# Attention scores on four row groups of the TensorE array, in three blocks per pair of heads

## The chip, the cores and the metric

The kernel runs on one core of a Trainium2 chip. The metric is the time of one execution on the device, in microseconds (us), as the median of three runs. A core has five engines that run their own instruction streams side by side and wait for one another by semaphores: TensorE (PE in the profile; its weight loads are shown apart as PEld), VectorE (DVE), ScalarE (ACT), GpSimd (POOL) and SyncE (SP), which here issues most of the DMA transfers.

## What is computed

Two stages. The first is attention restricted to equal hash buckets: a query sees the keys whose six sign bits under a random projection equal its own.

```python
batch, n_heads, seq, head_dim = (4, 8, 768, 64)
...
q_bits = (np.einsum('bhsd,dk->bhsk', q, proj) > 0).astype(np.int64)
k_bits = (np.einsum('bhsd,dk->bhsk', k, proj) > 0).astype(np.int64)
...
mask = q_bucket[:, :, :, None] == k_bucket[:, :, None, :]
scores = scale * np.matmul(q, k.transpose(0, 1, 3, 2))
scores = np.where(mask, scores, -1000000000.0)
scores = scores - np.max(scores, axis=-1, keepdims=True)
attn = np.exp(scores)
attn = attn / (np.sum(attn, axis=-1, keepdims=True) + 1e-09)
return np.matmul(attn, v).astype(np.float32)
```

The second stage takes the result as 3072 tokens of 512 numbers through a feed-forward block with 2048 hidden units and the quick form of gelu:

```python
h = x @ w_in
g = h * (1.0 / (1.0 + np.exp(-1.702 * h)))
return (g @ w_out).astype(np.float32)
```

All inputs and outputs are float32.

## The kernel before

Attention works on 16 pairs of heads (`pairs`, n = 0 to 15). The two heads of a pair lie in the two halves of the 128 partitions, 64 numbers of the head dimension each; j is the head within the pair. The 768 queries are taken in two halves c of 384 columns, the 768 keys in six tiles kt of 128. A PSUM tile `ps` spans two banks of 512 columns, one for each head.

The mask is not applied to scores. `hashed` (L405) multiplies projection and data and leaves the hash dots of q and k in one tile; `featured` (L414) turns their signs into bf16 numbers of size 2^16 in a small tile `f`, and eight DMA copies lay the rows of `f` out as features `feats[n % 2]`, 12 rows for each head. A product of these features is zero where all bits agree and hugely negative where one differs. `scores` (L426) adds both products in PSUM: for each key tile and head a bf16 matmul over the features (on 64 rows of the array, of which 12 hold numbers), then an f32 matmul over the head dimension (64 rows, and two passes on TensorE, each with its own weight load). The two heads use different halves of the array's rows. ScalarE then writes `es[c][:, kt]`, the exponential of the scaled sum (L436).

`values` (L453) multiplies v with these exponentials: 24 f32 matmuls for each c, each of 32 output columns of the array, four side by side. `unload` (L476) copies the result out of PSUM into `xT`. The sums of the exponentials over keys are made in two steps: `add_low` (L440) adds tiles 0 to 2 on GpSimd, `add_high` (L446) adds tiles 3 to 5 and the low sum on VectorE, and `total` (L482) adds over the 128 partitions with ones on TensorE, into `dn`. `invert` (L491) and `norm` (L507) divide by them on VectorE.

Data is prepared ahead: `fetch` (L320) loads q and k of pair n + 3, `turn` (L391) transposes those of pair n + 2 on VectorE, `measure` (L396) squares them on ScalarE and keeps the sum, for a check of sizes. Each pair also converts one chunk of the weights `w_in` (`convert`, L158: one 512 KB load `raw`, six steps on VectorE, one on ScalarE).

For a pair n from 1 on, the order is written out by hand. On TensorE: the scores of all six key tiles for c = 0, then for c = 1, then the values for c = 0 and for c = 1, the hash dots of pair n + 2, and the sums `total(n)`. The engines other than SyncE keep this order; SyncE's is made by the scheduler from it. In the profile of before SyncE issues, for each pair: eight feature copies (L423), the load of `raw` (L162), two loads of v (L343), four of k and four of q (L331). PSUM's eight banks are held by three pools: three places of two banks for `ps`, one bank for `av` and `dn`, one for hashes and the second `av`.

Of the kernel before, what the change touches and what calls it, by code (L numbers as in the profile page):

```python
# [38 lines left out]
def kernel(  # L39
# [246 lines left out]
    def attention(ff):  # L286
# [4 lines left out]
        with actx:  # L291
# [4 lines left out]
            aps = actx.enter_context(tc.tile_pool(name="aps", bufs=1, space=PSUM))  # L296
            mps = actx.enter_context(tc.tile_pool(name="mps", bufs=1, space=PSUM))
            early = actx.enter_context(ExitStack())
            ep = early.enter_context(tc.tile_pool(name="ep", bufs=1))
            sps = early.enter_context(tc.tile_pool(name="sps", bufs=GT, space=PSUM))  # L300
# [44 lines left out]
            def first_pair():  # L345
# [4 lines left out]
                for i, (name, src) in enumerate((("k", k), ("q", q))):  # L350
# [7 lines left out]
                    xts[0, name] = wk.tile([P, S], F32, tag=f"{name}T", name=f"{name}T")  # L358

                nc.scalar.activation(const.tile([1, 1], F32, name="first"), ones[0:1, 0:1], Act.Exp)  # L360
                for _ in range(4):
                    nc.tensor.matmul(aps.tile([P, 512], F32, tag="av", name="warm"), idle[:, 0:P], idle, start=True, stop=True)
                hash_weights()

                def turned(name, c, move):
                    tp = sps.tile([P, 2, 512], F32, tag="s", name="tp")[:, 0, 0:HS]
                    for i in range(GT):
                        for j in range(2):
                            nc.tensor.matmul(tp[D * j : D * (j + 1), i * P : (i + 1) * P], x[name][:, j, c * GT + i, :], ident,  # L369
                                             start=True, stop=True)  # L370
                    move(xts[0, name][:, c * HS : (c + 1) * HS], tp)

                def bits(name, c):
                    cols = slice(c * HS, (c + 1) * HS)
                    h = sps.tile([P, 2, 512], F32, tag="s", name="hash0")[:, 0, 0:HS]
# [13 lines left out]
                return lambda: bits("q", 1)  # L389

            def turn(n, name):  # L391
                x = raws[n, name]
                xt = xts[n, name] = wk.tile([P, S], F32, tag=f"{name}T", name=f"{name}T")
                nc.vector.transpose(xt, x.rearrange("p s i -> p (s i)"))

# [9 lines left out]
            def hashed(n):  # L405

                h = dots[n] = mps.tile([P, HS], F32, tag="m", name="hash")
# [6 lines left out]
            def featured(n):  # L414
                f = wk.tile([P, HS], BF16, tag="f", name="f", bufs=1)
                nc.vector.tensor_scalar(f, dots.pop(n), above[:, 0:1], weight[:, 0:1], op0=Alu.is_gt, op1=Alu.mult)
                for c in range(2):
                    for i, x in enumerate("kq"):

                        queue = nc.scalar if (n, x, c) == (1, "q", 0) else nc.sync  # L420
                        for j in range(2):
                            r0 = D * i + 32 * c + 2 * NB * j
                            queue.dma_start(out=feats[n % 2][x][D * j : D * j + 2 * NB, c * HS : (c + 1) * HS],  # L423
                                            in_=f[r0 : r0 + 2 * NB, :])

            def scores(n, c, kts):  # L426
                qT, kT, qf, kf = xts[n, "q"], xts[n, "k"], feats[n % 2]["q"], feats[n % 2]["k"]
                cols = slice(c * HS, (c + 1) * HS)
                for kt in kts:
                    ps = sps.tile([P, 2, 512], F32, tag="s", name="ps")  # L430
# [5 lines left out]
                    nc.scalar.activation(es[c][:, kt, :, 0:HS], ps[:, :, 0:HS], Act.Exp, scale=1.0 / D**0.5)  # L436
# [3 lines left out]
            def add_low(n, c):  # L440

                acc = accs[n, c, 0] = st.tile([P, 2, HS], F32, tag="acc0", name="acc0", bufs=1)
                nc.gpsimd.tensor_tensor(acc, es[c][:, 0, :, 0:HS], es[c][:, 1, :, 0:HS], op=Alu.add)  # L443
                nc.gpsimd.tensor_tensor(acc, acc, es[c][:, 2, :, 0:HS], op=Alu.add)  # L444

            def add_high(n, c):  # L446
                e = [es[c][:, GT + i, :, 0:HS] for i in range(GT)]
                acc = accs[n, c] = st.tile([P, 2, HS], F32, tag="acc", name="acc")
                nc.vector.scalar_tensor_tensor(acc, e[0], T * TINY, e[1], op0=Alu.add, op1=Alu.add)  # L449
                for x in (e[2], accs.pop((n, c, 0))):  # L450
                    nc.vector.tensor_tensor(acc, acc, x, op=Alu.add)  # L451

            def values(n, c, kts):  # L453
                if 0 in kts:


                    if c and n == 0 or c and n + 2 > last:
                        avs[n, c] = mps.tile([P, HS + 1], F32, tag="m", name="av")
                    elif c:
                        avs[n, c] = sps.tile([P, 2, 512], F32, tag="s", name="av1")[:, 0, 0 : HS + 1]  # L460
                    else:
                        avs[n, c] = aps.tile([P, HS + 1], F32, tag="av", name="av")
                av, vt = avs[n, c], vts[n]
# [18 lines left out]
            def total(n):  # L482

                dn = accs[n] = aps.tile([P, HS], F32, tag="av", name="dn")
# [6 lines left out]
            def invert(n):  # L491
# [7 lines left out]
                for r0 in range(0, P, 32):  # L499
# [5 lines left out]
                                    r.rearrange("p c s -> p (c s)").unsqueeze(2).to_broadcast([P, S // 32, 32]))  # L505

# [19 lines left out]
            def guard(part):  # L526
                if part == 0:
                    nc.vector.tensor_reduce(largest, sizes, axis=AX.X, op=Alu.max)
                else:
                    row = mps.tile([1, P], F32, tag="m", name="row")  # L530
                    nc.tensor.transpose(row, largest, ident)
                    nc.vector.tensor_reduce(largest[0:1, 0:1], row, axis=AX.X, op=Alu.max)
# [7 lines left out]
            scores(0, 0, low)  # L540
            rest()
            add_low(0, 0)
            scores(0, 0, high)
            turn(1, "k")
            measure(1, "k")
            values(0, 0, low)
            fetch(2, "k")
            scores(0, 1, low)
            add_low(0, 1)
            add_high(0, 0)  # L550
            turn(1, "q")
            measure(1, "q")
            values(0, 0, high)
            unload(0, 0)
            hashed(1)
# [3 lines left out]
            scores(0, 1, high)  # L559
            measure(2, "k")  # L560
            values(0, 1, low)
            values(0, 1, high)
            unload(0, 1)
            for n in range(1, last + 1):

                scores(n, 0, every)
                add_low(n, 0)
                if n == 1:
                    add_high(0, 1)
                    for x in "kq":  # L570
                        turn(2, x)
                    fetch(3, "k")
                    total(0)
                    measure(2, "q")
                    fetch(3, "q")
                    fetch_v(2)
                whole(invert(n - 1))
                norm(n - 1)
                if n == last:
                    guard(0)  # L580
                scores(n, 1, every)
                add_low(n, 1)
                add_high(n, 0)
                if n == 1:
                    hashed(2)
                    featured(2)
                if n + 2 <= last:
                    for x in "kq":
                        turn(n + 2, x)
                        measure(n + 2, x)  # L590
                if n == last:
                    guard(1)
                add_high(n, 1)
                values(n, 0, every)
                unload(n, 0)
                step(n, 6)
# [3 lines left out]
                if 1 < n < last:  # L600
                    fetch_v(n + 1)
                values(n, 1, every)
                unload(n, 1)
                if n + 2 <= last:
# [750 lines left out]
```

## Time and profile before

| | |
|---|---|
| median of three runs | 857.03 us (857.01 to 857.36) |
| the profiled execution | 856.89 us, of which the span from first to last instruction is 855.1 us |
| TensorE busy | 846.1 us, 99% of the span |
| VectorE busy | 701.5 us, 82% |
| ScalarE busy | 345.1 us, 40% |
| GpSimd busy | 357.1 us, 42% |
| granted TensorE clock | 0.998 |

The profile shows one execution. A group's row gives the source line, the engine, the operation, the tiles written and read, the shapes, a count, the busy time and the mean duration in ns of one, and then the engine's idle time before them with what ended it. In shapes such as 64\*128 64x384 the first pair is rows and columns of the array, the second the moving operand. A timeline row starts with the start in us from the begin of the span and the time from the first start to the last end of the instructions merged in it. A windows row gives a stretch, its length and the busy time of each engine in it, with the number of instructions in brackets. The chain of waits is followed back from the last instruction to whatever released it. Matmuls overlap in the array, so a matmul's duration is longer than its share of the time: the distance between starts counts.

### The profile page before, as it was taken

What the parts mean: (1) busy time and instruction counts of PE and PEld (TensorE: products, weight loads), DVE (VectorE), ACT (ScalarE), POOL (GpSimd) and SP (SyncE); (2) the same over time, 40 slices, a digit from 0 to 9 for tenths busy, and PEclk for the clock granted to TensorE, in tenths of its full rate; (3) what the DMA queues carried; (4) which work ended last, traced back from release to release, by engine and by line L of the source; (5) the groups of instructions that cost most, each with busy time, mean ns of one, the idle gap of its engine ahead of it and who ended that gap; (6) DMA issues with size and microseconds to landing.
All of it is one profiled execution on the core that took longest, in us unless ns stands there. A gap on an engine that the chain in (4) does not pass through costs nothing.

```text
span 855.1 us, 13646 instructions
## 1 busy us (share of the span) xinstructions
PE 846.1 (99%) x5007; PEld 529.1 (62%) x5007; DVE 701.5 (82%) x1069; ACT 345.1 (40%) x549; POOL 357.1 (42%) x316
## 2 busy tenths in 40 slices
PE   8999999999999999999999999999999999999996
PEld 4444444444444444566666666545888888888885
DVE  4489999999999885788887788676998977897786
ACT  5866666777766654343444444433000000000000
POOL 4333333433333358997854466668664100000000
PEclk9999999999999999999999999999999999999999
DMA  5635654444563103436565536587844675467534
GB/s 128 94 58 103 105 101 85 85 86 86 108 112 77 48 26 135 159 103 243 197 221 222 222 147 231 187 274 263 288 164 157 205 248 192 159 214 240 191 114 100
DMA packets 160903, 132.07 MB, mean 154 GB/s; under 512 B 122656, under 2 KB 137664, under 8 KB 155584
## 3 DMA queue, kind: packets, MB, share of 16 engines
q1 hardware_dynamic: 152448, 106.89, 44.6%
q10 hardware_dynamic: 8384, 24.27, 8.2%
q8 instruction: 40, 0.66, 0.3%
q14 instruction: 31, 0.25, 0.1%
HBM read 79.69 MB, written 50.33 MB: 152 GB/s over the span
## 4 chain that ended last, share of the span: by engine, by line
PE 98%; DMA 1%; ACT 0%; DVE 0%; ACTq 0%; issue 0%; DVEq 0%
PE product L1078 30%; PE product L751 23%; PE ps L435 18%; PE av L468 15%; PE small L819 6%; PE product L819 3%; PE dn L489 1%; PE hash L411 1%; DMA q<-in_q_dram 1%; PE hash L376 0%; PE tp L369 0%; ACT c L764 0%; DVE v L767 0%; ACT size L190 0%; DVE y L1058 0%
## 5 line engine op out<-in xcount | busy, mean ns | idle before, releaser
L436 ACT ACTIVATE e<-ps 128x768 f32<-128x768 f32 x192 | 151.2, 812 | 26.2 <-PE ps L435 23.6
L435 PE MATMUL ps<-qT,kT 64*128 64x384 f32 x768 | 155.1, 482 | 0.0
L443 POOL TENSOR_TENSOR acc<-e 128x768 f32<-128x768 f32 x32 | 51.6, 1613 | 195.1 <-ACT e L436 174.8
L468 PE MATMUL av<-e,v 128*32 128x385 f32 x1536 | 128.0, 487 | 0.0
L751 PE MATMUL product<-xT,w_in_sb 128*128 128x512 f32 x216 | 100.1, 593 | 0.1
L468 PEld LDWEIGHTS av<-e,v 128*32 128x32 f32 x1536 | 48.5, 109 | 76.3 <-issue 74.6
L435 PEld LDWEIGHTS ps<-qT,kT 64*128 64x128 f32 x768 | 68.0, 187 | 38.4 <-issue 38.4
L751 PE MATMUL product<-t_x,s_in 128*128 128x512 f32 x192 | 89.4, 592 | 0.0
L1114 ACT COPY u<-product 128x256 f32<-128x256 f32 x20 | 7.4, 372 | 158.4 <-PE product L1078 125.2
L751 PEld LDWEIGHTS product<-xT,w_in_sb 128*128 128x128 f32 x216 | 40.9, 190 | 36.5 <-issue 33.3
L435 PE MATMUL ps<-qf,kf 64*128 64x384 bf16 x384 | 62.8, 323 | 0.1
L444 POOL TENSOR_TENSOR acc<-acc,e 128x768 f32<-128x768 f32 x32 | 55.8, 1745 | 2.5
L751 PEld LDWEIGHTS product<-t_x,s_in 128*128 128x128 f32 x192 | 36.5, 190 | 29.7 <-issue 26.8
L449 DVE SCALAR_TENSOR_TENSOR acc<-e 128x768 f32<-128x768 f32 x32 | 47.7, 1490 | 5.1 <-ACT e L436 5.1
L767 DVE TENSOR_TENSOR u<-product,u 128x256 f32<-128x256 f32 (+1 forms) x60 | 28.4, 486 | 16.3 <-PE product L819 13.0
L435 PEld LDWEIGHTS <-kf 64*128 64x128 bf16 x384 | 18.9, 94 | 35.2 <-DMA q<-in_q_dram 6.2
L451 DVE TENSOR_TENSOR acc<-acc,e 128x768 f32<-128x768 f32 x32 | 34.3, 1072 | 3.3
L451 DVE TENSOR_TENSOR acc<-acc,acc 128x768 f32<-128x768 f32 x32 | 31.2, 974 | 6.6 <-POOL acc L444 3.2
L1078 PE MATMUL product<-raw_g,xT 128*128 128x256 f32 x152 | 35.1, 379 | 0.0
L767 DVE TENSOR_TENSOR v<-product,v 128x512 f32<-128x512 f32 x24 | 16.5, 689 | 20.0 <-PE product L751 20.0
L223 POOL TENSOR_TENSOR v<-c,v 128x1024 f32<-128x1024 f32 (+1 forms) x15 | 32.3, 2156 | 1.0
L222 POOL TENSOR_TENSOR u<-v,u 128x1024 f32<-128x1024 f32 (+1 forms) x11 | 23.8, 2163 | 20.7 <-ACT size L190 8.1
(284 smaller groups left out, 1721.9 us busy)
## 6 DMA issues: line engine op xcount, KB each, us to landing
raw_g<-g_dram SPq DMA_DIRECT2D x20, 1024.0 KB
s_in<-g_dram SPq DMA_DIRECT2D x20, 1024.0 KB
g_dram<-c ACTq DMA_DIRECT2D x18, 512.0 KB
raw<-in_moe_w_out_dram ACTq DMA_DIRECT2D x16, 512.0 KB
raw<-in_moe_w_in_dram SPq DMA_DIRECT2D x15, 512.0 KB
v<-in_v_dram SPq DMA_DIRECT2D x32, 192.0 KB
k<-in_k_dram SPq DMA_DIRECT2D x60, 96.0 KB
q<-in_q_dram SPq DMA_DIRECT2D x60, 96.0 KB
```

The lines of the kernel that those rows point to most:

```text
L223: lambda: eng.tensor_tensor(b12, b22, b12, op=Alu.subtract),
L435: nc.tensor.matmul(ps[:, j, 0:HS], a[hs, keys], m[hs, cols], start=not last, stop=last)
L436: nc.scalar.activation(es[c][:, kt, :, 0:HS], ps[:, :, 0:HS], Act.Exp, scale=1.0 / D**0.5)
L443: nc.gpsimd.tensor_tensor(acc, es[c][:, 0, :, 0:HS], es[c][:, 1, :, 0:HS], op=Alu.add)
L444: nc.gpsimd.tensor_tensor(acc, acc, es[c][:, 2, :, 0:HS], op=Alu.add)
L449: nc.vector.scalar_tensor_tensor(acc, e[0], T * TINY, e[1], op0=Alu.add, op1=Alu.add)
L451: nc.vector.tensor_tensor(acc, acc, x, op=Alu.add)
L468: nc.tensor.matmul(av[D * j + d : D * j + d + 32, :], vt[:, t, j, d : d + 32], es[c][:, t, j, :], start=(t == 0), stop=(t == T - 1))
L751: nc.tensor.matmul(ps, wq[LEFT[i]][:, kc, :], xq[RIGHT[i]][:, kc, :], start=(start and kc == 0), stop=(kc == K2 - 1), skip_group_check=not ...
L767: nc.vector.tensor_tensor(dst, x, y, op=Alu.add)
L819: nc.tensor.matmul(x, wq[LEFT[i]], xq[RIGHT[i]], start=start, stop=True, skip_group_check=True)
L1078: nc.tensor.matmul(ps, wq[LEFT[i]][:, c, :], gq[RIGHT[i]][:, c, :], start=(onto is None and c == 0), stop=(c == F4 - 1), skip_group_check= ...
```

## The change

The scores of a pair from 3 on take two key tiles at once. The array's rows are used in four groups of 32: group (j, i) holds head j and key tile i of the two. Since 32 rows hold only half of a head's 64 numbers, each f32 product is made in two steps, over `own` (the transposed q and k) and over `other`, a copy with the 32-row halves of each head exchanged. Four DMA copies for each pair make it (`exchange`); its places are `s_in`, which is not in use yet. The features are written to both 32-row groups of a head, by 16 copies instead of eight. Each of the four groups writes a PSUM bank of its own.

```diff
+            rooms = [s_in.rearrange("p i k f -> p (i k f)")[:, 2 * S * i : 2 * S * (i + 1)].rearrange("p (x s) -> p x s", s=S)
+                     for i in range(4)]
+            own = [wk.tile([P, 2, S], F32, name=f"own{i}", bufs=1) for i in range(2)] + rooms[3:]
+            other = rooms[:3]
+            low_sum = t_x[:, 2, :, 0:HS]
...
+            BY_PARTS = 3
...
+            def exchange(n):
+
+                for j in range(2):
+                    for i in range(2):
+                        r0, r1 = D * j + 32 * i, D * j + 32 * (1 - i)
+                        loader[0].dma_start(out=other[n % 3][r0 : r0 + 32], in_=own[n % 3][r1 : r1 + 32])
...
+                for part in range(2 if n >= BY_PARTS else 1):
+                    for c in range(2):
+                        for i, x in enumerate("kq"):
+
+                            queue = nc.scalar if (n, x, c) == (1, "q", 0) else nc.sync
+                            for j in range(2):
+                                r0 = D * i + 32 * c + 2 * NB * j
+                                r1 = D * j + 32 * part
+                                queue.dma_start(out=feats[n % 2][x][r1 : r1 + 2 * NB, c * HS : (c + 1) * HS],
+                                                in_=f[r0 : r0 + 2 * NB, :])
...
+            def scores_of_four(n, groups):
+
+                for c, k0 in groups:
+                    if n < BY_PARTS:
+                        scores(n, c, (k0, k0 + 1))
+                        continue
+                    cols = slice(c * HS, (c + 1) * HS)
+                    ps = [in_turn() for _ in range(2)]
+                    f, x, y = feats[n % 2], own[n % 3], other[n % 3]
+                    for at, (a, m) in enumerate(((f["k"], f["q"]), (x[:, 0], x[:, 1]), (y[:, 0], y[:, 1]))):
+                        for i in range(2):
+                            keys = slice((k0 + i) * P, (k0 + i + 1) * P)
+                            for j in range(2):
+                                r0 = D * j + 32 * i
+                                nc.tensor.matmul(ps[i][:, j, 0:HS], a[r0 : r0 + 32, keys], m[r0 : r0 + 32, cols],
+                                                 start=at == 0, stop=at == 2)
+                    for i in range(2):
+                        weigh(n, c, k0 + i, ps[i])
```

The pair's order changes too. The twelve score tiles come in three blocks of two groups of two tiles; between the first and second block stand the values of the pair before for c = 1, between the second and third those of this pair for c = 0, and after the third the hash dots of pair n + 2 and the sums of pair n − 1. PSUM is one pool of four places of two banks, given out in turn (`in_turn`) to scores, values and hashes. The low sums share one buffer, and their additions, those of `add_high` and the steps of the conversion are spread over the pair. `invert` and `norm` work on pair n − 2.

```diff
             for n in range(1, last + 1):

-                scores(n, 0, every)
+                if 1 < n < last:
+                    featured(n + 1)
+                if n > 2:
+                    inverse[n - 2] = invert(n - 2)
+                    next(inverse[n - 2])
+                scores_of_four(n, ((0, 0), (0, 2)))
+                add_high(n - 1, 1, (0, 1))
                 add_low(n, 0)
+                if n > 2:
+                    next(inverse[n - 2])
+                add_high(n - 1, 1, (2,))
+                if n > 2:
+                    norm(n - 2)
...
+                    if n + 2 <= last:
+                        measure(n + 2, "k")
+                    values(n - 1, 1, every, in_turn()[:, 0])
+                    unload(n - 1, 1)
+                if n < last:
+                    fetch_v(n + 1)
+                add_high(n, 0, (0,))
+                step(n, 2)
+                scores_of_four(n, ((0, 4), (1, 0)))
+                add_low(n, 1, (0,))
+                step(n)
+                add_high(n, 0, (1, 2))
...
+                    measure(n + 2, "q")
+                at = in_turn()
+                values(n, 0, every, at[:, 0])
...
+                if n + 2 <= last:
+                    for x in "kq":
+                        turn(n + 2, x)
+                    exchange(n + 2)
+                if n + 3 <= last:
+                    for x in "kq":
+                        fetch(n + 3, x)
+                scores_of_four(n, ((1, 2), (1, 4)))
+                add_low(n, 1, (1,))
+                step(n, 3)
                 if n < last:
+                    at = in_turn()
+                    if n + 2 <= last:
+                        hashed(n + 2, at[:, 0])
+                    if n > 1:
+                        total(n - 1, at[:, 1])
                     begin(n + 1)
```

For the last pair the values for c = 1, the sums and the size check follow after the loop. SyncE's order for a pair becomes: 16 feature copies for n + 1, two loads of v, one of k for n + 3, the four exchange copies for n + 2, the other three of k, four of q, and `raw`. Pair 0 keeps its order but takes its PSUM places from the new pool. Pairs 1 and 2 have the new order with the old matmuls.

More of the change, by code (lines that the diff above doesn't have):

```diff
@@ L446, in add_high @@
[L446 to L460, printed above, removed]
-                    else:
-                        avs[n, c] = aps.tile([P, HS + 1], F32, tag="av", name="av")
-                av, vt = avs[n, c], vts[n]
+                    weigh(n, c, kt, ps)
```

159 lines of the change are left out of this document (85 added, 74 removed).

## The prediction

> **What bounds the kernel now.** I read the page's shares and chain first, then the chain in order of time inside attention, then the engines one by one over a steady pair.
>
> ```profile
> span 855.1 us, 13646 instructions
> PE 98%; DMA 1%; ACT 0%; DVE 0%; ACTq 0%; issue 0%; DVEq 0%
> PE product L1078 30%; PE product L751 23%; PE ps L435 18%; PE av L468 15%; PE small L819 6%; PE product L819 3%; PE dn L489 1%; PE hash L411 1%; DMA q<-in_q_dram 1%; PE hash L376 0%; PE tp L369 0%; ACT c L764 0%; DVE v L767 0%; ACT size L190 0%; DVE y L1058 0%
> ```
> TensorE carries the chain almost alone. The change touches only attention, whose chain runs as follows:
>
> ```profile
> 184.50 0.65 PE dn L489 x8
> 185.14 9.80 PE ps L435 x72
> 194.94 7.90 PE av L468 x96
> 202.84 0.65 PE hash L411 x8
> 203.49 0.65 PE dn L489 x8
> ```
> From dn to dn a pair takes 203.49 − 184.50 = 18.99 us: scores 9.80, values 7.90, hashes 0.65, sums 0.65. Nothing waits in it. The engines over eleven such pairs, and over the one that I take as the pattern:
>
> ```profile
> core 0: us, PE busy (x) PEld busy (x) DVE busy (x) ACT busy (x) POOL busy (x), PEclk, DMA share, GB/s
> 70.37:279.26 208.89, 208.89 (x2029) 98.02 (x2024) 198.17 (x255) 146.17 (x233) 72.12 (x44) 1.00 0.50 93
> 203.30:222.29 18.99, 18.99 (x189) 8.89 (x184) 18.01 (x24) 13.28 (x23) 6.46 (x4) 1.00 0.51 97
> ```
> 208.89 / 11 is 18.99 again, at full clock. VectorE (18.01) is almost as full; ScalarE (13.28) and GpSimd (6.46) have room. This table has no column for SyncE, whose queue issues the loads. Its timeline for the same pair:
>
> ```profile
> 206.23 1.58 SPq L423 DMA_DIRECT2D kf<-f  x2
> 207.86 1.48 SPq L423 DMA_DIRECT2D qf<-f  x2
> 209.44 1.54 SPq L423 DMA_DIRECT2D kf<-f  x2
> 211.03 1.48 SPq L423 DMA_DIRECT2D qf<-f  x2
> 212.61 0.46 SPq L162 DMA_DIRECT2D raw<-in_moe_w_in_dram  x1
> 213.17 0.98 SPq L343 DMA_DIRECT2D v<-in_v_dram  x2
> 215.64 3.77 SPq L331 DMA_DIRECT2D k<-in_k_dram  x4
> 219.52 2.17 SPq L331 DMA_DIRECT2D q<-in_q_dram  x4
> 225.23 0.74 SPq L423 DMA_DIRECT2D kf<-f  x1
> kf<-f SPq DMA_DIRECT2D x4, 9.0 KB
> ```
> The eight feature copies hold the queue from 206.23 to 212.61: 6.4 us, 0.80 each, though each moves 9 KB. Then 0.56 for raw, 1.02 for v, 3.88 for k, 2.23 for q: 14.1 us of 19, and 4.9 us of waiting.
>
> **The change, part by part.** *Scores.* One key tile now, from bf16 phase to bf16 phase:
>
> ```profile
> 208.92 0.33 PE L435 MATMUL ps<-qf,kf 64*128 64x384 bf16 x2
> 209.08 0.81 PE L435 MATMUL ps<-qT,kT 64*128 64x384 f32 x4
> 209.73 0.33 PE L435 MATMUL ps<-qf,kf 64*128 64x384 bf16 x2
> L435 PEld LDWEIGHTS ps<-qT,kT 64*128 64x128 f32 x48 | 4.2, 187 | 2.5 <-issue 2.5
> L436 ACT ACTIVATE e<-ps 128x768 f32<-128x768 f32 x12 | 9.5, 812 | 1.3 <-PE ps L435 1.1
> ```
> The bf16 phase costs 0.16 us (208.92 to 209.08), the f32 phase 0.65, both heads at once; two tiles cost 1.62. After: one bf16 phase and two f32 phases for two tiles, 0.16 + 0.65 + 0.65 = 1.46, if four row groups run together as two do now. Bounds: 1.46, or 2.91 if only two overlap. I take 1.46: the values' 96 passes in 7.90 us are 0.33 per four, so four column groups already overlap fully; the weight loads (187 ns, in the shade of a pass of some 320) are per row group and stay hidden. Six groups a pair: −0.16 × 6 = −0.96 us.
>
> *Three blocks.* Scores and values now alternate, six switches of array shape a pair for two:
>
> ```profile
> 203.30 0.83 PE L489 MATMUL dn<-acc,ones 128*32 128x384 f32 x8
> 213.12 0.81 PE L435 MATMUL ps<-qT,kT 64*128 64x384 f32 x4
> 213.86 0.85 PE L468 MATMUL av<-e,v 128*32 128x385 f32 x8
> 222.29 0.83 PE L489 MATMUL dn<-acc,ones 128*32 128x384 f32 x8
> 223.06 0.34 PE L435 MATMUL ps<-qf,kf 64*128 64x384 bf16 x2
> ```
> An f32 phase is worth 0.65, so values at 213.86 come 0.09 late, and scores at 223.06 come 0.12 late after the sums' 0.65. Four more switches at 0.11 are +0.44. TensorE's pair becomes 18.99 − 0.96 + 0.44 = 18.47. ScalarE's four exponentials per block (0.81 each) catch up during the 3.95 us of values; its order costs nothing as long as data is there.
>
> *Features and exchange.* From pair 3 on the feature copies are 16, written twice for the two 32-row halves: +6.4 us on SyncE. Four exchange copies of 192 KB, SBUF to SBUF, are new. No row shows one; the nearest by size is raw (0.56 with its gap), the bounds are a store out of SBUF below and a feature copy above, 0.80:
>
> ```profile
> 333.68 0.32 SPq L761 DMA_DIRECT2D g_dram<-u  x1
> ```
> I take 0.45, nearer the large rows: +1.8 (1.3 to 3.2). The k row holds 1.6 us more than the q row for the same four copies; raw and v stand just ahead of it. Raw will now be issued behind q, but the exchange stands among the k copies, so I keep half: −0.8 (−1.6 to 0). SyncE's pair: 14.1 + 6.4 + 1.8 − 0.8 = 21.5 us, between 20.2 and 23.7. All of these exceed 18.47. This is the term that decides.
>
> *How it reaches TensorE.* The queue is strictly ordered: features for n+1, v, exchange for n+2 behind VectorE's transposes, k and q for n+3, raw. Late copies hurt in two places. The scores of n+1 need all row halves of their features at the start. And ScalarE now squares k of pair n+2 (measure) ahead of unloading the values, so a late k holds the unload, which holds a PSUM place of the next scores. Full bursts start in pairs 2 to 12, which is ten intervals. At the pattern's offset (206.23 is 2.9 after the dn at 203.30) I estimate that some 4 us of lag are absorbed before either wait bites (0 to 6). So the delay is 10 × (21.5 − 18.47) − 4 = +26.
>
> The Trainium skill, "DMA: Bandwidth & Descriptors", section "Issuing engines are not separate DMA queues", says that the sequencer time to start a DMA is usually small beside the transfer. By it SyncE would cost nothing. This trace disagrees: 0.80 us of queue for 9 KB.
>
> *The rest.* Sums a pair later, the low sums in a single buffer, and finer order on VectorE and GpSimd leave the number of operations as it was. Their risk is the shared work of VectorE and GpSimd:
>
> ```profile
> 208.41 1.69 POOL L444 TENSOR_TENSOR acc<-acc,e 128x768 f32<-128x768 f32 x1
> 215.67 1.70 POOL L444 TENSOR_TENSOR acc<-acc,e 128x768 f32<-128x768 f32 x1
> 209.10 1.81 DVE L509 TENSOR_TENSOR xT<-xT,rs 128x768 f32<-128x768 f32 x1
> 210.83 0.94 DVE L449 SCALAR_TENSOR_TENSOR acc<-e 128x768 f32<-128x768 f32 x1
> 215.74 2.44 DVE L449 SCALAR_TENSOR_TENSOR acc<-e 128x768 f32<-128x768 f32 x1
> ```
> The same L449 takes 0.94 free and 2.44 under a GpSimd add, ending 0.8 after it; the L509 multiply ends 0.8 after its own. VectorE is held 0.85 + 1.50 = 2.35 us a pair, so its own need is at most 18.99 − 2.35 = 16.6. Up to 1.8 us of holding (18.47 − 16.6) is covered even without SyncE's delay, up to 4.9 with it; beyond that each us costs one. A low add of the second half also waits for VectorE's use of the one buffer; behind it on GpSimd stand only more low adds. I count nothing. Pairs 1 and 2 keep the old matmuls and pay the switches, +0.9; the end, where sums follow the last values at once, +0.3 (−0.5 to +1).
>
> **The sum**, against the profiled execution (856.89, its span 855.1, and 0.14 below the median of 857.03): thirteen pairs × −0.52 = −6.8; pairs 1 and 2 and the end +1.2; SyncE's lag +26 less nothing for the pairs after, whose bursts are short. 856.9 + 20.4 = 877, the forecast. Ends: at 20.2 and 6 us of slack, 10 × 1.73 − 6 − 5.6 = +6, 863; at 23.7 and none, 52 − 5.6 = +47, 904.
>
> **Rivals.** *SyncE's queue doesn't bind* (0.19). If feature copies were issued in the time of a large one (raw, 0.56) and the exchange at the store's 0.32, the pair on SyncE would be 9.0 + 0.56 + 1.02 + 2.2 + 2.2 + 1.3 = 16.3, under 18.47: 856.9 − 5.6 = 851. For it: the queue idles 4.9 us now. Against: each of the eight rows above shows 0.74 to 0.80 with no wait to remove. It decides below 18.5 us a pair.
>
> *Four row groups don't overlap* (0.05), the change not doing what it says: at two a time a group is 2.91, TensorE's pair 18.47 + 6 × 1.45 = 27.2, over thirteen pairs +107: 963. Against it stand the values. The Trainium skill, "TensorE: Matmul & The Clock Gate", section "Measured speedup vs the span model", has 3.07 for four row tiles. By it a phase would take 4 / 3.07 = 1.30 times as long, an estimate that gives a pair of about 21.1, still inside SyncE's 21.5.
>
> *VectorE held by GpSimd* (0.05). If every GpSimd add (6.46 a pair) held VectorE in full, its pair would be 16.6 + 6.46 = 23.1, +4.1 over thirteen pairs: 910. It decides once the holding exceeds 4.9 us; two of four adds held it for 2.35 before.
>
> **How the numbers follow.** Forecast 0.68, SyncE free 0.19, no overlap 0.05, VectorE 0.05; 0.03 stays for gains and lag that cancel. A measurement of this kernel tells 0.2% (1.7 us) from no change. Faster 0.19, same 0.03, slower 0.78. The forecast's own range is 863 to 904; with the faster case taken in, and the top tenth left out, 849 to 897.
>
> **What would show it.** SyncE: no idle from pair 2 on, 16 feature copies in about 12.7 us, one burst 21 to 22 us. TensorE: key-tile pairs at 1.46 us, gaps of about 0.1 at each switch, then waits of 2 to 4 us in each pair from about pair 5, ended by ScalarE's unload behind the measure of k or by feature copies. Pairs 2 to 4 should run near 18.5. I am wrong if SyncE has idle time in pairs 5 to 12, if a score group takes more than 1.6, or if VectorE has no idle time while SyncE has.

## The result and the profile after

The changed kernel takes 938.63 us (median of four runs, 936.63 to 939.62) against 857.03: a ratio of 1.095, with an interval of 1.093 to 1.097. The forecast was 877, the range 849 to 897. It is slower, as forecast, but by 81.6 us and not by 20. About three quarters of that stand in the steady pairs, where the mechanism is the one that was forecast; the rest stands at the start, at the end and in the feed-forward part, where next to nothing was forecast.

The page of the changed kernel, its span, busy times and the chain by engine:

```profile
span 937.8 us, 15159 instructions
PE 873.4 (93%) x5631; PEld 531.6 (57%) x5631; DVE 705.2 (75%) x1069; ACT 336.0 (36%) x549; POOL 369.2 (39%) x316
PE 69%; SPq 12%; DMA 7%; DVE 6%; issue 3%; ACT 2%; ACTq 0%; DVEq 0%
```

The chain was 98% TensorE. Now SyncE's queue (SPq) and the DMAs hold 19% of it. SyncE's timeline for one turn of its queue, in a steady pair:

```profile
233.28 1.64 SPq L450 DMA_DIRECT2D kf<-f  x2
...
244.78 1.48 SPq L450 DMA_DIRECT2D qf<-f  x2
246.36 1.04 SPq L360 DMA_DIRECT2D v<-in_v_dram  x2
247.51 0.47 SPq L348 DMA_DIRECT2D k<-in_k_dram  x1
248.08 2.50 SPq L419 DMA_DIRECT2D s_in<-s_in  x4
250.63 3.07 SPq L348 DMA_DIRECT2D k<-in_k_dram  x3
253.79 2.98 SPq L348 DMA_DIRECT2D q<-in_q_dram  x4
256.87 0.58 SPq L162 DMA_DIRECT2D raw<-in_moe_w_in_dram  x1
257.55 0.78 SPq L450 DMA_DIRECT2D kf<-f  x1
```

Read the starts: each row begins about 0.1 us behind the end of the one before, or less, so the queue has next to no free time (SyncE's waits come to 13 us over ten such turns). From feature copy to feature copy is 257.55 − 233.28 = 24.27 us. Before, the same turn had 4.9 us of waiting in 19.

What that does to the rest: ScalarE's and TensorE's timelines around the middle of a pair.

```profile
226.95 1.51 ACT L454 ACTIVATE e<-s 128x768 f32<-128x768 f32 x2 [1.07 <-PE s L482]
233.27 0.84 ACT L426 ACTIVATE junk<-k 128x768 bf16<-128x768 f32 x1 [4.80 <-DMA q<-in_q_dram]
234.28 0.58 ACT L524 ACTIVATE xT<-s,vs 128x384 f32<-128x384 f32 x1
```

```profile
230.86 0.34 PE L482 MATMUL s<-qf,kf 32*128 32x384 bf16 x4
231.03 0.81 PE L482 MATMUL s<-own 32*128 32x384 f32 x8
231.67 0.81 PE L482 MATMUL s<-s_in 32*128 32x384 f32 x8
232.32 0.33 PE L482 MATMUL s<-qf,kf 32*128 32x384 bf16 x2
234.91 0.34 PE L482 MATMUL s<-qf,kf 32*128 32x384 bf16 x2 [2.27 <-ACT xT L524]
234.92 1.55 PE L482 MATMUL s<-own 32*128 32x384 f32 x8
236.13 1.62 PE L482 MATMUL s<-s_in 32*128 32x384 f32 x8
```

In brackets stands the idle time before an instruction and what ended it. ScalarE sits 4.80 us idle until a load of pair n + 2 has landed (the profile names q, the instruction reads k), squares it at 233.27, and only then unloads the values at 234.28. In ten pairs ScalarE sits idle ahead of its squares for 49.9 us, ten times, each time until a load of k or q lands. TensorE's second group needs the PSUM place behind that unload and stands 2.27 us. After the stop the two f32 phases take 1.21 us (234.92 to 236.13) and 1.55 us (to 237.68) instead of 0.64 each: from 234.90 to 238.10 the granted clock is 0.55. Undisturbed, a group of two tiles runs from 230.86 to 232.32, 1.46 us.

TensorE's waits over the whole run, by the instruction that waits and what ended it (us in total, times, longest), and the engines over ten pairs:

```profile
PE s L482 <- ACT xT L524: 27.6, 14, 3.5
PE s L482 <- DVE rt L539: 14.6, 12, 2.5
PE s L533 <- DVE acc L503: 5.5, 1, 5.5
```

```profile
core 0: us, PE busy (x) PEld busy (x) DVE busy (x) ACT busy (x) POOL busy (x), PEclk, DMA share, GB/s
99.62:342.93 243.31, 207.19 (x2322) 88.90 (x2314) 181.61 (x229) 125.76 (x211) 77.22 (x41) 0.94 0.60 110
```

The unload is the first wait. `rt`, which is VectorE's first read of the sums and frees another PSUM place, is the second. In ten pairs TensorE is idle for 36 us and runs at a clock of 0.94 where it had 1.00.

The changed kernel and the runs told of below can be laid out by four stretches, read from the starts of the first sums behind each pair (the `dn` rows; `s` at L533 in the changed kernel) and of the first product. Each entry is the difference to the profile of before (70.37, 227.24, 19.30 and 538.2 us):

| run | start, to the end of pair 2 | pairs 3 to 14 | pair 15 to the first product | feed-forward | sum |
|---|---|---|---|---|---|
| the change | +5.3 | +60.7 | +13.5 | +3.2 | +82.7 |
| order_alone | +3.3 | +5.8 | +12.5 | +1.9 | +23.5 |
| single_features | +5.9 | +6.6 | +13.9 | +1.6 | +28.1 |
| no_exchange | +5.3 | +11.6 | +13.5 | +1.9 | +32.3 |
| four_rows_alone | +4.4 | −0.2 | +13.5 | +2.1 | +19.8 |
| fewer_adds | +4.7 | −5.7 | +11.4 | +1.5 | +11.9 |
| start_end | +0.5 | −0.2 | +12.8 | +1.8 | +14.8 |
| few_copies | +4.2 | +56.3 | +12.9 | +3.0 | +76.4 |
| before_16 | +0.1 | +33.2 | +2.5 | −0.1 | +35.7 |
| features_pool | +6.0 | +16.9 | +16.9 | +1.9 | +41.7 |

In all rows but before_16 the values of c = 1 and the sums run a pair later, so 3.95 + 0.65 = 4.6 us of TensorE's work moved out of the first column into the third. Without that the start loses 9.9 in the changed kernel and the end 8.9.

### The profile page after: what moved, and what is told of

It is laid out like the page before. It is cut to its first block, busy times and chain, and to the rows that moved or that the text cites. A ratio compares the mean times of both kernels' runs of the same rounds, so it can differ in the third digit from the quotient of the medians.

```text
span 937.8 us, 15159 instructions
## 1 busy us (share of the span) xinstructions
PE 873.4 (93%) x5631; PEld 531.6 (57%) x5631; DVE 705.2 (75%) x1069; ACT 336.0 (36%) x549; POOL 369.2 (39%) x316
## 3 DMA queue, kind: packets, MB, share of 16 engines
q10 hardware_dynamic: 8384, 24.27, 7.7%
## 4 chain that ended last, share of the span: by engine, by line
PE 69%; SPq 12%; DMA 7%; DVE 6%; issue 3%; ACT 2%; ACTq 0%; DVEq 0%
PE product L1160 27%; PE product L833 21%; PE small L901 6%; SPq L348 6%; PE s L512 5%; PE s L482 4%; SPq L450 4%; PE product L901 3%; DMA q<-in_q_dram 3%; SPq L419 3%; PE s L465 2%; DMA raw<-in_moe_w_in_dram 1%; DMA qf<-f 1%; ACT junk L426 1%; DMA k<-in_k_dram 1%
## 5 line engine op out<-in xcount | busy, mean ns | idle before, releaser
L454 ACT ACTIVATE e<-s 128x768 f32<-128x768 f32 x192 | 144.9, 811 | 79.8 <-PE s L482 63.8
L493 POOL TENSOR_TENSOR t_x<-e 128x768 f32<-128x768 f32 x32 | 62.8, 1962 | 201.4 <-ACT e L454 150.9
L512 PE MATMUL s<-e,v 128*32 128x385 f32 x1536 | 135.6, 499 | 0.3 <-ACT e L454 0.3
L512 PEld LDWEIGHTS s<-e,v 128*32 128x32 f32 x1536 | 47.8, 111 | 87.2 <-issue 77.4
L482 PE MATMUL s<-s_in 32*128 32x384 f32 x816 | 88.2, 517 | 0.0
L503 DVE TENSOR_TENSOR acc<-acc,e 128x768 f32<-128x768 f32 x64 | 84.2, 1316 | 3.9
L493 POOL TENSOR_TENSOR t_x<-t_x,e 128x768 f32<-128x768 f32 x32 | 56.0, 1749 | 56.0 <-ACT e L454 54.7
L482 PE MATMUL s<-qf,kf 32*128 32x384 bf16 x312 | 35.8, 331 | 42.2 <-ACT xT L524 27.6
L482 PEld LDWEIGHTS s<-s_in 32*128 32x128 f32 x816 | 45.7, 196 | 19.2 <-issue 3.4
L833 PEld LDWEIGHTS product<-t_x,s_in 128*128 128x128 f32 x192 | 37.1, 193 | 31.1 <-issue 28.1
L482 PE MATMUL s<-own 32*128 32x384 f32 x432 | 51.0, 523 | 0.0
L426 ACT ACTIVATE junk<-k 128x768 bf16<-128x768 f32 x16 | 13.5, 842 | 58.2 <-DMA k<-in_k_dram 32.7
```

Of the source, the lines that this page charges most:

```text
L482: nc.tensor.matmul(ps[i][:, j, 0:HS], a[r0 : r0 + 32, keys], m[r0 : r0 + 32, cols], start=at == 0, stop=at == 2)
L493: nc.gpsimd.tensor_tensor(low_sum, low_sum if i else e[:, 0], e[:, i + 1], op=Alu.add)
L503: nc.vector.tensor_tensor(acc, acc, e[:, GT + i], op=Alu.add)
L512: nc.tensor.matmul(av[D * j + d : D * j + d + 32, :], vt[:, t, j, d : d + 32], es[c][:, t, j, :], start=(t == 0), stop=(t == T - 1))
L833: nc.tensor.matmul(ps, wq[LEFT[i]][:, kc, :], xq[RIGHT[i]][:, kc, :], start=(start and kc == 0), stop=(kc == K2 - 1), skip_group_check=not ...
```

## Experiments

The theory: SyncE's queue sets the pair, by the issue of twelve copies more (eight of features, four of the exchange). Rivals: the new order itself; the bytes of the exchange; a wait on VectorE that would stand there anyway. Every run is one execution with its profile; the kernel before took 856.55 to 856.97 us beside them.

**What the parts cost alone.** *e1_single_features* leaves out the second eight feature copies:

```diff
-                for part in range(2 if n >= BY_PARTS else 1):
+                for part in range(1):
```


> Leaves out the second eight feature copies of each pair from 3 on, so the second key tile of each group meets zero features (its scores are unmasked). Theory A (SyncE's queue sets the pair; it never idles and turns in 24.2 us: 13.1 for 16 feature copies, 1.1 v, 0.6 + 3.1 k, 2.6 exchange, 3.1 q, 0.6 raw): the queue's pair falls by 6.5 to about 17.7, under TensorE's 18.5, so pairs 3 to 14 fall from 24.0 to 18.5-19 and the time from 938.6 by some 63 to 870-880, with idle time on SyncE again. Theory B (the new order itself costs: TensorE's stops for PSUM places held by VectorE and ScalarE, and the half clock after each stop): pairs stay above 22, time above 915.

Measured 885.04, 5 us more than theory A allowed, with pairs of 19.5 us. *e2_no_exchange* leaves out the exchange and feeds the second f32 phase the first operands again:

```diff
-                    for at, (a, m) in enumerate(((f["k"], f["q"]), (x[:, 0], x[:, 1]), (y[:, 0], y[:, 1]))):
+                    for at, (a, m) in enumerate(((f["k"], f["q"]), (x[:, 0], x[:, 1]), (x[:, 0], x[:, 1]))):
...
-                    exchange(n + 2)
```


> Leaves out the four exchange copies; the second f32 phase multiplies the first phase's operands again. Theory A: SyncE's pair is 24.2 - 2.6 = 21.6 or less (k and q no longer share the DMA engines with the exchange), so twelve pairs save 2.4 or more each: 900-912. Theory B: within 5 us of 938.

Measured 889.23, 11 us under the range of theory A: over pairs 4 to 13 a pair falls from 24.3 to 20.1 us, by 4.2 where the exchange's own issue is 2.55. The loads of k and q get cheaper with it. *e3_order_alone* keeps the old matmuls and the old eight copies, in the new order:

```diff
-            BY_PARTS = 3
+            BY_PARTS = 16
...
-                    exchange(n + 2)
```


> The new order, PSUM places and sums a pair later, with the old matmuls for all pairs, eight feature copies and no exchange. Theory A: SyncE's pair is about 14-15, so TensorE sets it again: 18.99 + 0.44 for four more switches = 19.4, time about 938.6 - 12 x 4.6 = 880-885 if the slow first pairs and the slow end (together some 20 us) belong to the order. Theory B: 915 or more. If those 20 us belong to SyncE too: 862-868.

Measured 880.43, with pairs of 19.48 us. *e5_before_16* is the kernel before, its order and matmuls, with sixteen feature copies (the second set goes to rows that the 64-row matmuls read as well):

```diff
+                for part in range(2 if n >= 3 else 1):
+                    for c in range(2):
+                        for i, x in enumerate("kq"):
...
+                                r1 = D * j + 32 * part
+                                queue.dma_start(out=feats[n % 2][x][r1 : r1 + 2 * NB, c * HS : (c + 1) * HS],
```


> The kernel before with its features copied twice, also into 12 further rows of the 64 that its matmuls read (masked scores only become more negative). Nothing else changes. Theory A: SyncE's pair is 14.1 + 6.5 = 20.6, perhaps 21.3 with contention, against 18.99: ten intervals less some slack give 866-881, with no idle time on SyncE. Theory B (copies on SyncE are hidden): 857-860.

Measured 892.70, above the range of 866 to 881, with pairs of about 20 and 24 us in turn for the most part, 22.2 in the mean, with TensorE waiting 22.8 us in all for the unload. So the copies alone, with none of the order and none of the four row groups, cost 36 us. In the new order each set alone costs little over the run with neither (*four_rows_alone*, below, 876.79): the exchange 8.3, the second features 12.4, but both together 61.8. SyncE's waits show why. They come to 6.2 us a pair in *four_rows_alone*, to 4.4 with the exchange alone, to 1.5 with the second features alone and to 1.3 with both: the exchange fits into the free time, the features about fill it (pairs of 20.1), and only the sum goes far past it. *Order_alone* itself, which adds no copy, is 23.5 slower than before, and its pair only by 0.49.

**Issuing the copies elsewhere.** *e4_features_pool* issues the second feature copies from GpSimd:

```diff
-                            queue = nc.scalar if (n, x, c) == (1, "q", 0) else nc.sync
+                            queue = nc.gpsimd if part else nc.scalar if (n, x, c) == (1, "q", 0) else nc.sync
```


> The changed kernel, its second eight feature copies issued by GpSimd. SyncE's load is that of e1 (15.4 us of copies a pair), so if the load of SyncE alone sets the pair, e4 runs like e1, 880-890, pairs at 19.5. If it is the bytes and not the queue, or if GpSimd pays for the issue (low adds late, VectorE behind them), pairs go above 21 and the time above 900.

Measured 898.59: the same copies and bytes, 40 us less, because another engine issues them. It is not the rate of the bytes that held the pair: in ten pairs the DMA engines are busy for 0.72 of the time here and for 0.60 in the changed kernel. The time lies between the two expectations, and the pairs stay at 20.5 us. GpSimd's and VectorE's timelines (here of the run with the start and end edits too, same copies) show why:

```profile
218.47 1.05 POOL L450 DMA_DIRECT2D kf<-f  x2 [3.17 <-DVE f L441]
219.51 1.03 POOL L450 DMA_DIRECT2D qf<-f  x2
220.54 1.03 POOL L450 DMA_DIRECT2D kf<-f  x2
221.56 1.03 POOL L450 DMA_DIRECT2D qf<-f  x2
222.60 1.55 POOL L493 TENSOR_TENSOR t_x<-e 128x768 f32<-128x768 f32 x1
```

```profile
222.67 2.31 DVE L503 TENSOR_TENSOR acc<-acc,e 128x768 f32<-128x768 f32 x1
224.91 2.43 DVE L554 TENSOR_TENSOR xT<-xT,rs 128x768 f32<-128x768 f32 x1
...
229.57 1.92 DVE L186 TENSOR_TENSOR w_in_sb<-bits,mask_ff 128x512 uint32<-128x512 uint32 x1
```

Eight copies hold GpSimd 4.1 us, 0.52 each, and its adds stand behind them. SyncE has 4.7 us of waits a pair again; VectorE has almost none (0.5 us in 205). Its rows beside GpSimd's adds are held: those shown take 0.95, 0.94 and 0.69 us when nothing runs beside them. With a fourth (L193, 1.26 where 0.64 is free) that is 4.7 us a pair (3.5 in *four_rows_alone*, below). TensorE's stops in these pairs end with VectorE's `rt`.

*e10_few_copies* leaves SyncE its old eight copies. The second set becomes four copies from the first set's rows, issued by ScalarE, and GpSimd issues the exchange:

```diff
-                        loader[0].dma_start(out=other[n % 3][r0 : r0 + 32], in_=own[n % 3][r1 : r1 + 32])
+                        nc.gpsimd.dma_start(out=other[n % 3][r0 : r0 + 32], in_=own[n % 3][r1 : r1 + 32])
...
-                for part in range(2 if n >= BY_PARTS else 1):
+                for part in range(1):
...
+            def doubled(n):
+                for x in "kq":
+                    for j in range(2):
+                        r0, r1 = D * j, D * j + 32
+                        nc.scalar.dma_start(out=feats[n % 2][x][r1 : r1 + 2 * NB], in_=feats[n % 2][x][r0 : r0 + 2 * NB])
...
                 unload(n, 0)
                 if n == 1:
                     featured(2)
+                if BY_PARTS - 1 <= n < last:
+                    doubled(n + 1)
```


> The whole change, but SyncE issues only the eight old feature copies; the second set is four copies from the first set's rows, issued by ScalarE, and the four exchange copies are issued by GpSimd. SyncE's theory: its queue falls to about 14 us a pair, ScalarE's rises by some 3 to about 16, GpSimd's by 2.1 to 8.6, all under TensorE's 18.5; the pairs should run as in the run without either set of copies, 18.5 to 19.5 us, and the run ends at 868 to 882. Rival (the bytes of the exchange and not their issue cost the time): pairs stay above 20 us, with waits for features or loads, and the run ends above 890.

Measured 933.42, a miss: almost nothing was gained, and pairs 3 to 14 take 23.6 us each, as the rival had it. ScalarE's timeline and SyncE's, in this run:

```profile
233.43 1.57 ACTq L457 DMA_DIRECT2D kf<-kf  x2
235.10 2.03 ACTq L457 DMA_DIRECT2D qf<-qf  x2
237.23 2.92 ACT L460 ACTIVATE e<-s 128x768 f32<-128x768 f32 x4 [3.30 <-DMA k<-in_k_dram]
```

```profile
234.08 2.67 SPq L348 DMA_DIRECT2D k<-in_k_dram  x4
236.85 6.22 SPq L348 DMA_DIRECT2D q<-in_q_dram  x4
```

I had counted ScalarE's busy time (13 of 18.5 us) and not its place in the chain: the four issues take 3.7 us (0.9 each) straight ahead of the exponentials of the third block (they are the 3.30 us of idle time that the profile puts down to a DMA), whose PSUM places TensorE waits for next. Over the run TensorE waits 25.8 us for exponentials and 16.3 us for the doubled features to land. And q's four loads, with no exchange on their queue, take 6.22 us to issue instead of 2.2. The doubled features and the exchange had just been issued on other queues; which of the two held q up was not told apart. SyncE itself waits 9.7 us a pair here, so this run neither confirms nor refutes that SyncE's issue is the price of the exchange: for the features *features_pool* parts issue from bytes, for the exchange no run does. A copy's price is not only its own issue.

**Start and end.** *e6_tail* moves the last high sums ahead of the last steps of the conversion; *e7_pool_tail* does that in the run with GpSimd's copies; *e8_pool_tail_start* adds that in pair 1 VectorE transposes pair 3 ahead of dividing pair 0, and ScalarE measures pair 3 behind the unload:

```diff
                 add_low(n, 1, (1,))
+                if n == last:
+                    add_high(last, 1)
                 step(n, 3)
...
-            add_high(last, 1)
             x_sums[3]()
```

The edit of the start:

```diff
-                if n + 2 <= last:
-                    for x in "k" if n == 1 else "":
-                        measure(n + 2, x)
+                if 1 < n <= last - 2:
                     measure(n + 2, "q")
...
-                if n in (1, last):
+                if n == last:
                     whole(invert(n - 1))
                     norm(n - 1)
...
                         turn(n + 2, x)
+                        if n == 1:
+                            measure(n + 2, x)
                     exchange(n + 2)
+                if n == 1:
+                    whole(invert(n - 1))
+                    norm(n - 1)
```


> The changed kernel with one edit at the end: the high sums of the last pair stand on VectorE ahead of the last conversion steps and of the sums for the feed-forward part. Theory (the end is VectorE's order, not SyncE): the 5.5 us that TensorE waits for the last sums go, and with them some of the 10.2 us at half clock that follow: 928-934. If the end was SyncE's lag: within 2 us of 938.6.

> e4 and e6 together: if both are separate, e4's time less what e6 saves: 873-882.

> e7, and in pair 1 the squares of pair 3 after the unload on ScalarE, its transposes ahead of the first inversion on VectorE. Theory: pair 1 loses some 7 us of TensorE to these two orders (stops of 3.5 for the transposes and 1.5 for a PSUM place, then 3.4 us at half clock): 4 to 7 less than e7. If pair 1 waits for SyncE's loads instead: no change.

Measured 937.07, 898.43 and 894.48: the end's edit gives 1.6 (inside the spread of the changed kernel's four runs, 3.0) and 0.2, the start's 4.0. The first two missed their ranges, the third reached the lower end of its own. The stop of 5.5 us for `acc` in the end became three, 1.6 for `acc`, 1.8 for the size check and 2.8 for `rt`: VectorE has no room there (busy for 29.7 of the last 32.8 us before the first product), and a stop only moves. SyncE's lag, the other reading of *e6_tail*, is out: *four_rows_alone* (below), with SyncE's queue free, loses the same 13.5 in this stretch. The start's edit shortened a stop and, with it, removed a stretch of halved clock (0.50 from 51 to 58 us in the run without the edit, 1.00 with it).

**What would be left with a free queue.** *e9_four_rows_alone* leaves out both sets of copies and keeps the four row groups:

```diff
-                for part in range(2 if n >= BY_PARTS else 1):
+                for part in range(1):
...
-                    for at, (a, m) in enumerate(((f["k"], f["q"]), (x[:, 0], x[:, 1]), (y[:, 0], y[:, 1]))):
+                    for at, (a, m) in enumerate(((f["k"], f["q"]), (x[:, 0], x[:, 1]), (x[:, 0], x[:, 1]))):
...
-                    exchange(n + 2)
```


> Neither the second set of feature copies nor the exchange; the matmuls on four row groups stay (pairs from 3 on see unmasked scores in every second key tile, and the second f32 phase repeats the first operands). SyncE's queue then needs about 14 us a pair. If SyncE is the only bound of the changed kernel, a pair falls to TensorE's own 18.5 us (1.0 less than the 19.48 of the new order with the old matmuls) and the run ends near 868. Rival: a PSUM place that VectorE frees late (hashes and sums of the pair before) holds the second group of each pair by about 0.9 us whatever the queue does; then pairs stay at 19.3 to 19.6 and the run ends near 880, so that the four row groups would give nothing even with a free queue.

Measured 876.79, with pairs of 19.00 us, between the two expectations for a pair and nearer the rival's in the end time. Its TensorE and VectorE, over eight pairs and in one:

```profile
112.48:264.50 152.02, 150.77 (x1861) 66.33 (x1857) 147.48 (x185) 101.44 (x169) 56.91 (x33) 1.00 0.50 95
```

```profile
207.07 2.00 DVE L200 SCALAR_TENSOR_TENSOR w_in_sb<-raw,w_in_sb 128x512 f32<-128x512 f32 x1
208.99 0.67 DVE L441 TENSOR_SCALAR f<-s,above,weight 128x384 bf16<-128x384 f32 x1
209.58 0.57 DVE L539 STREAM_TRANSPOSE rt<-s 128x384 f32<-128x384 f32 x1
...
214.16 1.88 DVE L503 TENSOR_TENSOR acc<-acc,e 128x768 f32<-128x768 f32 x1
...
219.74 3.17 DVE L503 TENSOR_TENSOR acc<-acc,e 128x768 f32<-128x768 f32 x2
```

```profile
209.72 0.33 PE L482 MATMUL s<-qf,kf 32*128 32x384 bf16 x2
210.20 0.34 PE L482 MATMUL s<-qf,kf 32*128 32x384 bf16 x2 [0.15 <-DVE rt L539]
```

VectorE is busy 147.48 of 152.02 us, and its rows stand end to end: `rt` comes when the row of L200 is done, and TensorE's second group waits for it. *e11_fewer_adds* tests that this is the second bound: in the same run it also leaves out two of VectorE's adds a pair:

```diff
                 for i in parts:
+                    if i == 2:
+                        continue
```


> The run with neither set of copies again (876.8, pairs of 19.00 us), and on VectorE the last add of each half's exponentials (key tile 5) left out, two adds a pair, so that the sums lack one tile of six. If VectorE's stream, almost without a gap in that run, is the second bound behind SyncE, a pair falls from 19.00 to TensorE's own 18.6 and the run ends 5 us or more earlier, near 870. Rival (TensorE itself is the bound at 19.0, its groups or switches being longer than counted): the pairs stay at 19.0 and the run loses only what the end had on VectorE, 1 to 3 us.

Measured 868.84, with pairs of 18.52 us and no wait for `rt` left in them. VectorE is the second bound, at 19.00; TensorE's own pair is 18.52. A steady group in this run, TensorE's timeline:

```profile
212.49 0.34 PE L482 MATMUL s<-qf,kf 32*128 32x384 bf16 x4
212.67 1.46 PE L482 MATMUL s<-own 32*128 32x384 f32 x16
213.96 0.33 PE L482 MATMUL s<-qf,kf 32*128 32x384 bf16 x4
```

*e12_start_end* is *four_rows_alone* with the start and end edits:

> The run with neither set of copies (876.8), with two edits of order: in pair 1 VectorE transposes pair 3 ahead of inverting and dividing pair 0 and ScalarE measures pair 3 behind the unload; in the last pair the last high sums stand ahead of the last three steps of the conversion. If the 20 us that this run still loses against before sit in the start (4.4), the end (13.5) and the first products (2.1), as its trace says, and come from VectorE's order there, these edits give back 4 to 7 us: 870 to 873. Rival: VectorE has no room left at the end, so that a stop only moves, and the edits give back the start's 4 us at most: 872 to 876.

Measured 871.69, inside the first expectation's range, but the table divides it as the rival has it: the start gives back 3.9, the end 0.7. No run beat the kernel before. Even with a queue that carried nothing new, start, end and feed-forward lose 15.1 in the last of these runs, and the pairs 3 to 14 of *fewer_adds* gain 5.7.

## Why the prediction was wrong, and where it was right

*What decides.* "SyncE's pair: 14.1 + 6.4 + 1.8 − 0.8 = 21.5 us, between 20.2 and 23.7. All of these exceed 18.47. This is the term that decides." Right in kind: the queue has next to no gap, the unload behind the measure of k ends most of TensorE's waits, and issuing eight copies from another engine gives 40 us back. The size is the step that failed: the pair of SyncE measures 24.27, above the upper bound too. By terms, from the starts in the row of SyncE: features 13.08 (12.8 forecast), v 1.15 (1.02), raw 0.68 (0.56), the exchange 2.55 (1.8), k 0.57 + 3.16 = 3.73 (3.1), q 3.08 (2.23). Of the 2.8 us that were missing, 0.75 are the exchange's. It was priced by the raw load and a store; an exchange copy measures 0.64 with its gap, inside the bounds 0.32 to 0.80. Another 1.5 are that k and q were priced as if nothing moved beside them. "I keep half: −0.8" had k get cheaper when raw is no longer ahead of it; instead k stayed nearly as dear as before (3.88), and q went from 2.23 to 3.08. The exchange around them goes with it: without it, in *no_exchange*, a load of k takes 0.57 us of SyncE and one of q 0.66 in the mean over ten turns, against 0.81 and 0.82 in the changed kernel. How 768 KB of exchange hold up these loads is not shown.

*The absorbed lag.* "Some 4 us of lag are absorbed" and "pairs 2 to 4 should run near 18.5" failed. Pair 2, still with the old matmuls, ran from 56.19 to 76.39 without a stop, 20.2 us at a clock of 0.96; pair 3 took 99.62 − 75.63 = 23.99 us already, and all of pairs 3 to 14 24.0 in the mean. SyncE's timeline of the start shows that the bursts for pairs 2 and 3 follow each other:

```profile
48.66 1.53 SPq L450 DMA_DIRECT2D kf<-f  x2
...
60.28 2.57 SPq L348 DMA_DIRECT2D q<-in_q_dram  x4
62.96 1.65 SPq L450 DMA_DIRECT2D kf<-f  x2
...
87.47 1.67 SPq L450 DMA_DIRECT2D kf<-f  x2
```

From 62.96 the turn is 24.5 us at once, and the lag is there before pair 3 begins. With 24.27 and no slack the prediction's own formula would have given 10 × 5.8 − 5.6 = 52; the measured +60.7 in pairs 3 to 14 is 12 × (24.00 − 18.94): twelve pairs were late and not ten, and none of the 4 us of slack showed.

*TensorE's part* was right: 1.46 us for a group, four row groups in full overlap, and 18.47 forecast against 18.52 (*fewer_adds*). *Order_alone* shows the switches, 19.48 against 18.99 + 0.44. The rival in which four row groups don't overlap is out: with the queue and VectorE out of the way, an f32 phase of four groups takes no longer than one of two did, 0.65 us. The Trainium skill's 3.07 for four row tiles ("TensorE: Matmul & The Clock Gate", "Measured speedup vs the span model") gave an estimated pair of 21.1 us. The trace does not bear that out, at 18.52.

*Issue time.* The Trainium skill's rule that issuing is usually small beside the transfer ("DMA: Bandwidth & Descriptors", "Issuing engines are not separate DMA queues") would have cost SyncE nothing. The trace disagrees as it did before: 16 feature copies take 13.08 us of the queue.

*"Sums a pair later ... I count nothing", and the start and end at +1.2.* These steps failed too, hidden behind the larger miss: start, end and feed-forward together are +22.0 in the changed kernel. *Order_alone* costs 23.5 us, of which pairs 3 to 14 are 5.8; *four_rows_alone* still costs 19.8 with a pair no longer than before. At the end VectorE has two divisions and all late sums left when TensorE runs out of scores; at the start VectorE's order delays pair 3. Both make TensorE stop (5.46 and 3.52 us), and both stops were followed by a halved clock. In the steady pairs of *four_rows_alone*, VectorE's rows are held longer than before by GpSimd's adds: 3.17 for two and 1.88 for one add, 2.00 for L200, where the free rows take about 0.95 and 0.69. That is 1.27 + 0.93 + 1.31 = 3.5 us a pair, against 2.35 before, which makes 19.00 the pair that VectorE allows. The prediction had the warning in its own figures: it covered 1.8 us of holding without SyncE's delay, and its rows showed 2.35. So VectorE, with GpSimd's holding in it, is the second bound; the rival "VectorE held by GpSimd", with 4.9 us of holding and more, did not come about.

*"SyncE's queue doesn't bind": 851.* Wrong twice: it binds, and with its load taken away the kernel takes 876.8, not 851, because of the start and the end in the new order and of VectorE's pair of 19.00.

## What to carry to other kernels

Price a copy on the queue that issues it, by a row of that queue, and add the price that it puts on the copies beside it: a queue with 5 us free took either of two new sets at little cost, and not both. When work is moved a step later to smooth a loop, draw up the start and the end as carefully as the steady pair; there the moved work has nothing to hide behind. And before an engine is made faster, look which engine comes next: here VectorE needed 19.00 us a pair and TensorE's new pair 18.52, so a gain of 0.5 us could not show even with a free queue.

## What the runs showed of the hardware

- Of the ten stops of TensorE of more than 2.4 us in the changed kernel, eight were followed by a granted clock of about one half, most for some 3.4 us. In the run with sixteen copies in the old order, long and short stops take turns; its windows behind a stop of 2.61 us and behind one of 1.60 (PEclk is the third column from the end):

```profile
249.20:252.40 3.20, 3.20 (x16) 1.96 (x17) 3.01 (x7) 2.43 (x4) 1.77 (x2) 0.57 1.49 155
271.60:274.80 3.20, 3.20 (x24) 2.05 (x25) 2.99 (x7) 3.20 (x5) 1.71 (x2) 1.00 1.35 163
```

It is not a fixed rule: in the changed kernel the clock stayed at 1.00 behind the stops of 2.54 us at 137.35 and 2.96 us at 308.49, and it was halved behind one of 2.13 us at 210.95. It was halved in eight of the twelve pairs 3 to 14, and from 392.2 to 402.4, around the end of the stop of 5.46 us and behind it; the first product begins at 396.44, so this is part of the feed-forward's +3.2.

- Issuing a copy of 9 KB on 12 partitions takes 0.71 us on SyncE and 0.52 on GpSimd, one of 192 KB on 32 partitions 0.58 on SyncE. The groups of the changed kernel (minimum, median and maximum in ns):

```profile
L450 SPq DMA_DIRECT2D qf<-f x79: 713/714/1197, 99.2 to 341.3; - x79
L419 SPq DMA_DIRECT2D s_in<-own x24: 565/582/742, 126.0 to 299.2; - x24
```

The smaller copy is the dearer one to issue: here the issue time does not follow the bytes.
